# Decode attention with feed-forward: groups of eight heads with two loads for K and V each, and w_gate loaded in three pieces

## The chip, the cores and the metric

The kernel runs on one core of a Trainium2 chip. The metric is device time in microseconds (us) of one execution. Before the change it is 189.06 us (median of four runs, 188.81 to 189.14), so a difference of half a microsecond can be told. Each profile is one execution, whose span is 1.2 to 1.9 us shorter than the time of the same run. On one core a run is marked slow when it is over 1.5% above the fastest run of the same kernel; ratios below use fast runs only.

## The reference, cut to what matters

Two sequences, one new token each. The parts that move bytes are 32 heads of K and V (the last 1,024 positions of each, 192 values per position, bf16) and the weights.

```python
W = min(4096, max(256, Sk // 4))             # 1024
q = (x @ wq).reshape(B, Sq, Hq, Dh)...       # 2 x 32 heads x 192
k = k_cache[:, :, Sk - W:, :]                # v the same
p = softmax(einsum('bhqd,bhkd->bhqk', q, k) * Dh ** -0.5)
o = einsum('bhqk,bhkd->bhqd', p, v) ... @ wo
...                                          # adaLN around both halves
_gelu(x @ w_gate) * (x @ w_up) @ w_down
```

The kernel reads 76.88 MB in all, each byte once. K and V are 50 MB of that (their caches are four times as large; the rest isn't read).

## The kernel before

All large loads are issued by one queue, in one fixed order, into a ring of eight slots and into a region for the other weights. A K or V load brings 128 rows of 12,288 bytes (32 positions of one head), one row to each SBUF partition. The line that says which row goes to which partition:

```python
HQ = 4; PH = P // HQ          # 4 heads in a group, 32 blocks of positions
J = W // PH                   # 32 positions in a block
NQD = H // HQ; NG = B * NQD   # 8 quads, 16 groups
...
quad, b = group(i)
src = A_k_cache if kind == "k" else A_v_cache
return src[b].rearrange("(i u) s d -> u i s d", u=NQD)[quad, :, K0:Sk, :] \
             .rearrange("i (p j) d -> p i (j d)", p=PH), SLOT
```

Read as nested counts, the source is 32 blocks outside, 4 heads inside, 6,144 elements in a row; the destination is 128 partitions. So partition 4p + i gets block p of head i. The head step is 12 MiB, the block step 12,288 bytes.

w_gate is one load of 128 rows:

```python
S.dma("sp", k_dma(wg_v..., B_w_gate.rearrange("(p k) n -> p (k n)", k=KT)), sem_wg, ...)
```

For each group the vector engine multiplies K with q (two multiplies of 128 x 3,072), the matrix engine adds up products, and a chain of small steps makes the softmax.

## Time and profile before

| kernel before | |
|---|---|
| time, median | 189.06 us |
| HBM bytes read | 76.88 MB |
| mean rate over the span | 410 GB/s |
| a 12,288-byte packet on its DMA engine | 464.5 ns |
| vector multiplies | 32 x 1.75 us = 56 us |

From the page of the kernel before: the DMA rows of the 40 slices (busy tenths of the 16 DMA engines, and GB/s), the chain that ended last, the group of the large multiplies (busy us, mean ns, idle us before them and what ended it), and three DMA issues (count, size of one, median us from issue to landing).

```profile
DMA  7999998999999999999999999999999999999991
GB/s 254 402 451 435 430 459 372 422 435 424 430 422 422 427 425 426 427 424 420 419 432 432 422 423 422 421 438 422 424 423 422 419 488 428 416 384 442 398 396 45
...
DMA 71%; DVE 15%; PE 7%; ACT 2%; SPq 2%; issue 1%
...
L490 DVE TENSOR_TENSOR prod<-ring,qbc 128x3072 bf16<-128x3072 bf16 x32 | 55.9, 1751 | 14.3 <-DMA ring<-in_A_k_cache_dram 14.3
...
ring<-in_A_k_cache_dram SPq DMA_DIRECT2D x16, 1536.0 KB, 24.4
ring<-in_A_v_cache_dram SPq DMA_DIRECT2D x16, 1536.0 KB, 24.2
...
r<-in_B_w_gate_dram SPq DMA_DIRECT2D x1, 1920.0 KB, 25.0
```

The DMA engines are busy almost everywhere, at about 425 GB/s. The time from issue to landing is long only because several loads are always queued ahead.

One more reading comes from the trace's records of landings, which the page does not print. A load's 16 parts mark their completion one by one. In the last load of the kernel before, the 16 marks lie between 182.92 and 184.75 us, a spread of 1.83 us. I read each mark as one engine's, since there are 16 of both and the spread comes back in the three loads ahead (1.95, 1.94 and 1.87 us): the engines do not finish together.

### The profile page before, as it was taken

Reading aid. Unit: us, or ns where it says so; the run is one execution under the profiler, and the core shown is the slowest. Engines: PE = TensorE matmul, PEld = TensorE weight load, DVE = VectorE, ACT = ScalarE, POOL = GpSimd, SP = SyncE. Lnnn points to the kernel's source line nnn. Section 1 sums busy time; section 2 is a strip of 40 time slices with the busy share of each in tenths; the row PEclk is TensorE's granted clock in tenths of the full one; section 3 lists DMA queues with packets and bytes.
Section 4 is the critical chain, followed back from the end, with each engine's and each line's share of the span. In section 5 each row is a group of like instructions: output and inputs, shape, how many; then the busy total and the mean of one; then the engine's idle time right before and its main releaser. Section 6 shows DMA issues by size and latency. Waiting matters only on the chain.

```text
span 187.6 us, 2409 instructions
## 1 busy us (share of the span) xinstructions
PE 107.5 (57%) x1039; PEld 51.1 (27%) x1039; DVE 98.2 (52%) x147; ACT 29.9 (16%) x72; POOL 5.1 (3%) x23
## 2 busy tenths in 40 slices
PE   0014730742968887676676655675497395364462
PEld 0011200210323443333423323233253152353121
DVE  6131100019588988886595695775865933003211
ACT  3041100082001221112011110210120103103400
POOL 8200000000000000000000000000000000000000
PEclk9999999997587999999879999999969967569696
DMA  7999998999999999999999999999999999999991
GB/s 254 402 451 435 430 459 372 422 435 424 430 422 422 427 425 426 427 424 420 419 432 432 422 423 422 421 438 422 424 423 422 419 488 428 416 384 442 398 396 45
DMA packets 6518, 77.03 MB, mean 411 GB/s; under 512 B 746, under 2 KB 876, under 8 KB 1516
## 3 DMA queue, kind: packets, MB, share of 16 engines
q1 hardware_dynamic: 6492, 76.88, 97.1%
q8 instruction: 8, 0.13, 0.3%
q10 hardware_dynamic: 16, 0.01, 0.0%
q14 instruction: 2, 0.02, 0.0%
HBM read 76.88 MB, written 0.00 MB: 410 GB/s over the span
## 4 chain that ended last, share of the span: by engine, by line
DMA 71%; DVE 15%; PE 7%; ACT 2%; SPq 2%; issue 1%
DMA ring<-in_A_k_cache_dram 37%; DMA ring<-in_A_wq_dram 17%; DMA r<-in_B_w_down_dram 17%; DVE prod L490 9%; PE ps L502 4%; DVE S_sb L509 4%; PE ps L467 2%; SPq L266 2%; ACT qbc L483 2%; DVE ps L485 1%; DVE M L512 1%; ACT qrow L474 1%; PE ps L526 0%; DVE bcR L519 0%; PE ps L684 0%
## 5 line engine op out<-in xcount | busy, mean ns | idle before, releaser
L490 DVE TENSOR_TENSOR prod<-ring,qbc 128x3072 bf16<-128x3072 bf16 x32 | 55.9, 1751 | 14.3 <-DMA ring<-in_A_k_cache_dram 14.3
L502 PE MATMUL ps<-prod,ident_b 128*128 128x512 bf16 x192 | 52.9, 419 | 14.4 <-DVE prod L490 14.4
L502 PEld LDWEIGHTS ps<-prod,ident_b 128*128 128x128 bf16 x192 | 17.5, 104 | 40.2 <-DVE prod L490 17.5
L509 DVE TENSOR_REDUCE S_sb<-ps 128x32 f32<-128x1024 f32 x16 | 19.3, 1206 | 2.1 <-PE ps L502 2.1
L526 PE MATMUL ps<-bcR,bcL 5*128 5x4 f32 x32 | 6.1, 258 | 21.9 <-DVE bcR L519 21.9
L563 ACT ACTIVATE On<-ps,rden 128x384 bf16<-128x384 f32 x16 | 9.3, 580 | 43.5 <-DVE rden L561 21.1
L551 PE MATMUL ps<-ring,E_sb 128*8 128x384 bf16 x256 | 15.5, 369 | 0.0
L534 ACT ACTIVATE E_sb<-Sb_sb 128x128 bf16<-128x128 f32 x16 | 5.0, 310 | 56.4 <-DVE Sb_sb L531 56.4
L467 PE MATMUL ps<-ring,hT 128*2 128x512 bf16 x60 | 6.7, 626 | 9.8 <-DMA ring<-in_A_wq_dram 8.8
L526 PEld LDWEIGHTS ps<-bcR,bcL 5*128 5x128 f32 x32 | 4.7, 183 | 26.1 <-DVE bcR L519 26.1
L477 DVE CAST qrow<-ps 128x512 bf16<-128x512 f32 x1 | 0.7, 692 | 15.7 <-PE ps L467 15.7
L622 PE MATMUL ps<-ring,oT 128*17 128x160 bf16 x192 | 5.5, 294 | 5.6 <-DMA ring<-in_A_wo_dram 5.6
L531 DVE TENSOR_TENSOR Sb_sb<-S_sb,ps 128x128 f32<-128x128 f32 x16 | 4.6, 287 | 7.6 <-PE ps L526 7.6
L540 PEld LDWEIGHTS ps<-denp,maskc 128*128 128x128 f32 x32 | 7.1, 224 | 3.7 <-ACT E_sb L534 0.9
L641 DVE TENSOR_TENSOR lnt<-ps,modR 128x160 f32<-128x160 f32 x1 | 0.3, 325 | 12.6 <-PE ps L622 12.6
L445 PE MATMUL ps<-r,scT 128*17 128x480 bf16 x40 | 4.3, 597 | 3.9 <-DMA r<-in_w_mod_dram 3.9
L622 PEld LDWEIGHTS ps<-ring,oT 128*17 128x17 bf16 x192 | 4.9, 117 | 6.2 <-DMA ring<-in_A_wo_dram 6.2
L551 PEld LDWEIGHTS ps<-ring,E_sb 128*8 128x8 bf16 x256 | 5.1, 90 | 3.7 <-issue 1.2
L396 PE MATMUL ps<-st,selstat 128*128 128x2 f32 x4 | 0.9, 298 | 8.6 <-ACT sqj L392 8.6
L467 PEld LDWEIGHTS ps<-ring,hT 128*2 128x2 bf16 x60 | 1.7, 114 | 14.7 <-DMA ring<-in_A_wq_dram 9.7
L576 PE MATMUL ps<-On,zsel 128*128 128x96 bf16 x64 | 5.2, 241 | 0.7 <-ACT On L563 0.7
L540 PE MATMUL ps<-denp,maskc 128*128 128x1 f32 x32 | 5.1, 230 | 0.8 <-ACT E_sb L534 0.8
(81 smaller groups left out, 71.2 us busy)
## 6 DMA issues: line engine op xcount, KB each, us to landing
ring<-in_A_k_cache_dram SPq DMA_DIRECT2D x16, 1536.0 KB, 24.4
ring<-in_A_v_cache_dram SPq DMA_DIRECT2D x16, 1536.0 KB, 24.2
r<-in_w_mod_dram SPq DMA_DIRECT2D x1, 4800.0 KB, 14.3
ring<-in_A_wq_dram SPq DMA_DIRECT2D x1, 4608.0 KB, 32.3
ring<-in_A_wo_dram SPq DMA_DIRECT2D x1, 4480.0 KB, 23.4
ring<-in_A_wq_dram SPq DMA_DIRECT2D x1, 3072.0 KB, 21.2
ring<-in_A_wo_dram SPq DMA_DIRECT2D x1, 2720.0 KB, 24.1
r<-in_B_w_gate_dram SPq DMA_DIRECT2D x1, 1920.0 KB, 25.0
```

Of the source, the lines that this page charges most:

```text
L467: last = e.matmul(ps[32 * i:32 * i + B, n, :], lhsT=hT[:, k, :], rhs=wv[:, kk, i, n * QW:(n + 1) * QW], start=(k == 0), stop=(k == KT - 1) ...
L490: S.op("dve", lambda e: e.tensor_tensor(out=prod[:, 2 * (g % 2) + ci, :, :], in0=ring[:, sl, ci * JC * Dh:(ci + 1) * JC * Dh].rearrange("p ...
L502: last = e.matmul(o_ap, lhsT=ident_b[:, :], rhs=prod[:, pz, :, t * GC:(t + 1) * GC], start=(t == 0), stop=(t == NCH - 1))
L509: S.op("dve", lambda e: e.tensor_reduce(out=S_sb[:, z, :], in_=ps[:, 2 * z:2 * z + 2, :].rearrange("p k (j c) -> p (k j) c", c=GC), axis=A ...
L526: S.op("pe", lambda e: e.matmul(ps[:, BK_T, P:P + HQ], lhsT=bcL[:, :], rhs=bcR[:, z, :], start=True, stop=True), reads=[("bcR", z), "bcL"] ...
L531: S.op("dve", lambda e: e.tensor_tensor(out=Sb_sb[:, z, :, :], in0=S_sb[:, z, :].unsqueeze(2).broadcast_to([P, J, HQ]), in1=ps[:, BK_T, P: ...
L534: S.op("act", lambda e: e.activation(out=E_sb[:, z, :, :], in_=Sb_sb[:, z, :, :], func=ACTF.Exp, scale=SCALE, accum_out=denp[:, z:z + 1]), ...
L540: S.op("pe", lambda e: e.matmul(ps[:, BK_T, P + 16:P + 17], lhsT=maskc[:, :], rhs=denp[:, z:z + 1], start=True, stop=True), reads=[("denp" ...
L551: last = e.matmul(ps[32 * i:32 * i + 2 * HQ, BK_O, 0:ON], lhsT=E_sb[:, z, 2 * jp:2 * jp + 2, :].rearrange("p j h -> p (j h)"), rhs=ring[:, ...
L563: S.op("act", lambda e: e.activation(out=On[:, quad % 2, b, :], in_=ps[:, BK_O, 0:ON], func=ACTF.Identity, scale=rden[:, z:z + 1]), reads= ...
L576: last = e.matmul(ps[:, BK_OT, 0:B * NT].rearrange("p (b t) -> p b t", b=B), lhsT=zsel[:, jj, x:x + P], rhs=On[:, quad % 2, :, jj * Dh + d ...
L622: last = e.matmul(ps[32 * i:32 * i + RM, BK_M, 0:DR], lhsT=oT[:, t, :], rhs=wv[:, tl, i, :], start=(t == 0), stop=(t == NT - 1), tile_posi ...
```

## The change

Its intent is twofold. First, eight heads share one pass of small softmax steps, which halves their number. For this a partition holds 64 positions of one of eight heads, and these 64 come in two loads of 32, so that a load keeps its size. Second, w_gate is loaded in two pieces of eight rows and one of 112, meant to give one half of the 16 DMA engines nine of its rows and the other half seven, to even out their finish. (In the trace of the changed kernel each eight-row piece leaves eight landing marks and the 112-row piece 16; which engines these are no record says.)

```diff
-    HQ = 4
+    HQ = 8
     PH = P // HQ
     J = W // PH
+    JS = 32
+    NSUB = J // JS
...
+    WG_SPLIT = [(112, 120), (120, 128), (0, 112)]
...
-        items += [("k", 0)]
-        for g in range(1, NG):
-            items += [("k", g), ("v", g - 1)]
+        items += [("k", sq) for sq in range(NSUB)]
+        for sq in range(NSUB, NG * NSUB):
+            items += [("k", sq), ("v", sq - NSUB)]
...
-            return src[b].rearrange("(i u) s d -> u i s d", u=NQD)[quad, :, K0:Sk, :].rearrange("i (p j) d -> p i (j d)", p=PH), SLOT
+            return src[b].rearrange("(h u) s d -> u h s d", u=NQD)[quad, :, K0:Sk, :].rearrange("h (x s j) d -> s x h (j d)", x=PH, s=NSUB)[sub], SLOT
...
-        S.dma("sp", k_dma(wg_v..., B_w_gate...), sem_wg, writes=["wg"], ...)
+        for ci, (p0, p1) in enumerate(WG_SPLIT):
+            S.dma("sp", k_dma(wg_d[p0:p1, :], wg_s[p0:p1, :]), sem_wg[ci], writes=[("wg", ci)], ...)
```

The source of a K or V load is now 16 blocks outside and 8 heads inside. There are still 128 rows of 12,288 bytes, now with a block step of 24,576 bytes and a head step of 6 MiB. The rest of the diff (cut here) adapts the selection matrices, the order of the loop and the spread of q to eight heads.

More of the change, by code (lines that the diff above doesn't have):

```diff
@@ L149, in bass_adaLN_cond__sliding_block_cached__geglu_ffn__decode_kernel @@
     NG = B * NQD
+    V = HQ // NR
+    JS = 32
+    NSUB = J // JS
     NT = NQ // P
@@ L155, in bass_adaLN_cond__sliding_block_cached__geglu_ffn__decode_kernel @@
     assert DD * NT == Dh and DD * H == P and NR * FR == FC and FC * P == F and DR == KT * 32
-    assert HQ == NR and DD * NQD == 32
+    assert V * NR == HQ and JS * NSUB == J and 2 * HQ <= 32
     SCALE = float(Dh) ** -0.5
@@ L160, in bass_adaLN_cond__sliding_block_cached__geglu_ffn__decode_kernel @@
     JC = 16
-    NCK = J // JC
+    NCK = JS // JC
     GC = 512 // JC
@@ L165, in bass_adaLN_cond__sliding_block_cached__geglu_ffn__decode_kernel @@
     ON = 2 * Dh
-    NPAIR = J // 2
+    NPAIR = JS // 2
     NS = 8
-    SLOT = J * Dh
+    SLOT = JS * Dh
     WQ_SPLIT = [(0, 2), (2, 3)]
@@ L177, in bass_adaLN_cond__sliding_block_cached__geglu_ffn__decode_kernel @@
     HP = P // 2
-    X0 = DD * NQD - 1
+    HS = DD * NQD
+    X0 = HS - 1
     ZW = X0 + P
@@ L182, in bass_adaLN_cond__sliding_block_cached__geglu_ffn__decode_kernel @@
     FT = F // NR
-    assert NQB * QW == NQD * Dh
+    UW = min(2, NQD)
+    QU = UW * Dh
+    NQU = NQD // UW
+    assert NQB * QW == NQ // NR == V * NQD * Dh
     MH = 3 * DR
@@ L211, in bass_adaLN_cond__sliding_block_cached__geglu_ffn__decode_kernel @@
         selrow = sb("selrow", [P, NR, B], BF16)
-        selq = sb("selq", [P, B, P], BF16)
+        selq = sb("selq", [P, B, V, P], BF16)
         ztmp = sb("ztmp", [P, NR, 2, HQ], BF16)
@@ L258, in bass_adaLN_cond__sliding_block_cached__geglu_ffn__decode_kernel @@
         sem_wm = S.sem("d_wm")
-        sem_wg = S.sem("d_wg")
+        sem_wg = [S.sem("d_wg%d" % i) for i in range(len(WG_SPLIT))]
         sem_wu = [S.sem("d_wu%d" % i) for i in range(len(WU_SPLIT))]
@@ L268, in bass_adaLN_cond__sliding_block_cached__geglu_ffn__decode_kernel @@
         items = [("wq", k) for k in range(NWQ)]
-        items += [("k", 0)]
-        for g in range(1, NG):
-            items += [("k", g), ("v", g - 1)]
-        items += [("v", NG - 1)]
+        items += [("k", sq) for sq in range(NSUB)]
+        for sq in range(NSUB, NG * NSUB):
+            items += [("k", sq), ("v", sq - NSUB)]
+        items += [("v", sq) for sq in range((NG - 1) * NSUB, NG * NSUB)]
         items += [("wo", i) for i in range(NWO)]
@@ L302, in ring_src @@
                 return A_wo.rearrange("(p t) n -> p (t n)", t=NT)[:, t0 * D:(t0 + n) * D], n * D
-            quad, b = group(i)
+            g, sub = divmod(i, NSUB)
+            quad, b = group(g)
             src = A_k_cache if kind == "k" else A_v_cache
-            return src[b].rearrange("(i u) s d -> u i s d", u=NQD)[quad, :, K0:Sk, :].rearrange("i (p j) d -> p i (j d)", p=PH), SLOT
+            return src[b].rearrange("(h u) s d -> u h s d", u=NQD)[quad, :, K0:Sk, :].rearrange("h (x s j) d -> s x h (j d)", x=PH, s=NSUB)[sub], SLOT
         def declare_ring(consumed=()):
@@ L341, in bass_adaLN_cond__sliding_block_cached__geglu_ffn__decode_kernel @@
              reads=["ones_b"], writes=["selg"], name="selg")
+        S.op("pool", lambda e: e.memset(selq[:, :, :, :], 0.0), writes=["selq"], name="selq0")
         for b in range(B):
-            S.op("pool", lambda e, b=b: e.affine_select(out=selq[:, b, :].rearrange("p (x h) -> p x h", h=HQ),
-                                                        in_=ones_b[:, 0:1].unsqueeze(2).broadcast_to([P, PH, HQ]),
-                                                        pattern=[[0, PH], [-32, HQ]],
-                                                        compare_op=ALU.is_equal, fill=0.0, base=-b, channel_multiplier=1),
-                 reads=["ones_b"], writes=[("selq", b)], name="selq%d" % b)
+            for v in range(V):
+                S.op("pool", lambda e, b=b, v=v: e.affine_select(out=selq[:, b, v, :].rearrange("p (x i v) -> p x i v", i=NR, v=V)[:, :, :, v],
+                                                                 in_=ones_b[:, 0:1].unsqueeze(2).broadcast_to([P, PH, NR]),
+                                                                 pattern=[[0, PH], [-32, NR]],
+                                                                 compare_op=ALU.is_equal, fill=0.0, base=-b, channel_multiplier=1),
+                     reads=["ones_b"], writes=["selq"], name="selq%d_%d" % (b, v))
         S.op("pool", lambda e: e.affine_select(out=ztmp[:, :, :, :].rearrange("p i q h -> p i (q h)"),
@@ L433, in bass_adaLN_cond__sliding_block_cached__geglu_ffn__decode_kernel @@
              reads=["mask_h"], writes=["maskc"], name="maskc")
-        S.op("dve", lambda e: e.tensor_reduce(out=zsel[:, :, X0:X0 + P].rearrange("p q (h m) -> p q h m", m=32)[:, :, :, 0],
+        S.op("dve", lambda e: e.tensor_reduce(out=zsel[:, :, X0:X0 + P].rearrange("p q (h m) -> p q h m", m=HS)[:, :, :, 0],
                                               in_=ztmp[:, :, :, :].rearrange("p i q h -> p q h i"), axis=AX.X, op=ALU.max),
@@ L478, in bass_adaLN_cond__sliding_block_cached__geglu_ffn__decode_kernel, with f @@
                      reads=[bank(n)], writes=[("qrow", n)], name="q1_evac%d" % n)
-        for u, (n, b) in enumerate((n, b) for n in range(NQB) for b in range(B)):
-            bk = BK_T + u % 4
-            S.op("pe", lambda e, n=n, b=b, bk=bk: e.matmul(ps[:, bk, :], lhsT=selq[:, b, :], rhs=qrow[:, n * QW:(n + 1) * QW], start=True, stop=True),
-                 reads=[("selq", b), ("qrow", n)], writes=[bank(bk)], name="q2_%d_%d" % (n, b))
-            S.op("act", lambda e, n=n, b=b, bk=bk: e.activation(out=qbc[:, b, n * QW:(n + 1) * QW], in_=ps[:, bk, :], func=ACTF.Copy),
+        for z, (n, b) in enumerate((n, b) for n in range(NQU) for b in range(B)):
+            bk = BK_T + z % 4
+            def f(e, n=n, b=b, bk=bk):
+                last = None
+                for v in range(V):
+                    o0 = NQD * Dh * v + n * QU
+                    last = e.matmul(ps[:, bk, 0:QU], lhsT=selq[:, b, v, :], rhs=qrow[:, o0:o0 + QU], start=(v == 0), stop=(v == V - 1))
+                return last
+            S.op("pe", f, reads=["selq"] + [("qrow", m) for m in range(NQB)], writes=[bank(bk)], name="q2_%d_%d" % (n, b))
+            S.op("act", lambda e, n=n, b=b, bk=bk: e.activation(out=qbc[:, b, n * QU:(n + 1) * QU], in_=ps[:, bk, 0:QU], func=ACTF.Copy),
@@ L484, in bass_adaLN_cond__sliding_block_cached__geglu_ffn__decode_kernel, with d_mul @@
                  reads=[bank(bk)], writes=[("qbc", b, n)], name="q2_evac%d_%d" % (n, b))
         S.op("dve", lambda e: e.memset(ps[:, 5:8, :], 0.0), writes=[bank(k) for k in range(5, 8)], name="init_O2")
-        def d_mul(g, ci):
-            quad, b = group(g)
-            sl = slot_of[("k", g)]
-            S.op("dve", lambda e: e.tensor_tensor(out=prod[:, 2 * (g % 2) + ci, :, :],
+        def d_mul(sq, ci):
+            quad, b = group(sq // NSUB)
+            sl = slot_of[("k", sq)]
+            pz = 2 * (sq % 2) + ci
+            S.op("dve", lambda e: e.tensor_tensor(out=prod[:, pz, :, :],
@@ L491, in d_mul @@
                                                   in0=ring[:, sl, ci * JC * Dh:(ci + 1) * JC * Dh].rearrange("p (j d) -> p j d", d=Dh),
                                                   in1=qbc[:, b, quad * Dh:(quad + 1) * Dh].unsqueeze(1).broadcast_to([P, JC, Dh]), op=ALU.mult),
-                 reads=[("ring", sl)] + [("qbc", b, n) for n in range(quad * Dh // QW, ((quad + 1) * Dh - 1) // QW + 1)], writes=[("prod", 2 * (g % 2) + ci)], name="mul%d_%d" % (g, ci))
-        def p_reduce(g, ci):
-            pz = 2 * (g % 2) + ci
+                 reads=[("ring", sl), ("qbc", b, quad // UW)], writes=[("prod", pz)], name="mul%d_%d" % (sq, ci))
@@ L498, in f, with p_reduce @@
+        def p_reduce(sq, ci):
+            pz = 2 * (sq % 2) + ci
             def f(e):
@@ L504, in f, with c_sum, c_max @@
                 return last
-            S.op("pe", f, reads=[("prod", pz), "ident_b"], writes=[bank(pz)], name="red%d_%d" % (g, ci))
-        def c_sum(g):
+            S.op("pe", f, reads=[("prod", pz), "ident_b"], writes=[bank(pz)], name="red%d_%d" % (sq, ci))
+        def c_sum(sq):
+            g, sub = divmod(sq, NSUB)
+            z, w = g % 2, sq % 2
+            S.op("dve", lambda e: e.tensor_reduce(out=S_sb[:, z, sub * JS:(sub + 1) * JS], in_=ps[:, 2 * w:2 * w + 2, :].rearrange("p k (j c) -> p (k j) c", c=GC),
+                                                  axis=AX.X, op=ALU.add),
+                 reads=[bank(2 * w), bank(2 * w + 1)], writes=[("S", z)], name="sum_%d" % sq)
+        def c_max(g):
             z = g % 2
-            S.op("dve", lambda e: e.tensor_reduce(out=S_sb[:, z, :], in_=ps[:, 2 * z:2 * z + 2, :].rearrange("p k (j c) -> p (k j) c", c=GC),
-                                                  axis=AX.X, op=ALU.add),
-                 reads=[bank(2 * z), bank(2 * z + 1)], writes=[("S", z)], name="sum_%d" % g)
             S.op("dve", lambda e: e.tensor_reduce(out=M1[:, z:z + 1], in_=S_sb[:, z, :], axis=AX.X, op=ALU.max),
@@ L541, in p_den, with p_pv @@
                  reads=[("denp", z), "maskc"], writes=[bank(BK_T)], name="den_%d" % g)
-        def p_pv(g):
+        def p_pv(sq):
+            g, sub = divmod(sq, NSUB)
             z = g % 2
-            sl = slot_of[("v", g)]
+            sl = slot_of[("v", sq)]
             def f(e):
@@ L550, in f @@
                     i = jp % NR
+                    j0 = sub * JS + 2 * jp
                     last = e.matmul(ps[32 * i:32 * i + 2 * HQ, BK_O, 0:ON],
-                                    lhsT=E_sb[:, z, 2 * jp:2 * jp + 2, :].rearrange("p j h -> p (j h)"),
+                                    lhsT=E_sb[:, z, j0:j0 + 2, :].rearrange("p j h -> p (j h)"),
                                     rhs=ring[:, sl, 2 * jp * Dh:(2 * jp + 2) * Dh],
-                                    start=(jp < NR), stop=(jp >= NPAIR - NR), tile_position=(0, 32 * i))
+                                    start=(sub == 0 and jp < NR), stop=(sub == NSUB - 1 and jp >= NPAIR - NR), tile_position=(0, 32 * i))
                 return last
-            S.op("pe", f, reads=[("E", z), ("ring", sl)], writes=[bank(BK_O)], name="PV_%d" % g)
+            S.op("pe", f, reads=[("E", z), ("ring", sl)], writes=[bank(BK_O)], name="PV_%d" % sq)
         def c_rec(g):
@@ L581, in p_sel @@
             S.op("pe", f, reads=[("On", quad % 2, bb) for bb in range(B)] + ["zsel"], writes=[bank(BK_OT)], name="sel_%d" % quad)
-        for g in range(NG + 2):
+        for sq in range((NG + 1) * NSUB + 1):
+            g, sub = divmod(sq, NSUB)
             has = g < NG
             prev = 1 <= g <= NG
-            pp = g >= 2
+            head = sub == 0
+            pp = g >= 2 and head
             if has:
-                d_mul(g, 0)
-                p_reduce(g, 0)
+                d_mul(sq, 0)
+                p_reduce(sq, 0)
             if pp:
                 c_rec(g - 2)
-            if prev:
-                c_sum(g - 1)
+            if 1 <= sq <= NG * NSUB:
+                c_sum(sq - 1)
+            if prev and head:
+                c_max(g - 1)
             if has:
-                d_mul(g, 1)
-                declare_ring([("k", g)])
-            if prev:
+                d_mul(sq, 1)
+                declare_ring([("k", sq)])
+            if prev and head:
                 c_max2(g - 1)
@@ L600, in bass_adaLN_cond__sliding_block_cached__geglu_ffn__decode_kernel @@
             if has:
-                p_reduce(g, 1)
-            if prev:
+                p_reduce(sq, 1)
+            if prev and head:
                 c_exp(g - 1)
@@ L607, in bass_adaLN_cond__sliding_block_cached__geglu_ffn__decode_kernel @@
             if prev:
-                p_pv(g - 1)
-                declare_ring([("v", g - 1)])
+                p_pv(sq - NSUB)
+                declare_ring([("v", sq - NSUB)])
         S.op("act", lambda e: e.activation(out=oT[:, :, 0:RM:RB].rearrange("p t b -> p b t"),
@@ L629, in bass_adaLN_cond__sliding_block_cached__geglu_ffn__decode_kernel @@
         r3_dead = [wm_dma] + mod_pe
-        S.dma("sp", k_dma(wg_v.rearrange("p k n -> p (k n)"), B_w_gate.rearrange("(p k) n -> p (k n)", k=KT)), sem_wg,
-              writes=["wg"], deps=r3_dead, name="ld_wg")
+        wg_d, wg_s = wg_v.rearrange("p k n -> p (k n)"), B_w_gate.rearrange("(p k) n -> p (k n)", k=KT)
+        for ci, (p0, p1) in enumerate(WG_SPLIT):
+            S.dma("sp", k_dma(wg_d[p0:p1, :], wg_s[p0:p1, :]), sem_wg[ci], writes=[("wg", ci)], deps=r3_dead, name="ld_wg%d" % ci)
         for ci, (k0, nk) in enumerate(WU_SPLIT):
@@ L657, in f @@
                     return last
-                S.op("pe", f, reads=["ln2_out", key], writes=[bank(bk)], name="ffn_%s%d" % (name, ci))
-        ffn_gu(0, wg_v, "gate", [(0, KT, "wg")])
+                S.op("pe", f, reads=["ln2_out"] + key, writes=[bank(bk)], name="ffn_%s%d" % (name, ci))
+        ffn_gu(0, wg_v, "gate", [(0, KT, [("wg", ci) for ci in range(len(WG_SPLIT))])])
         S.op("act", lambda e: e.activation(out=gl[:, :], in_=ps[:, 0, 0:FT], func=ACTF.Gelu_apprx_tanh),
              reads=[bank(0)], writes=["gl"], name="gelu")
-        ffn_gu(1, wu_v, "up", [(k0, nk, ("wu", ci)) for ci, (k0, nk) in enumerate(WU_SPLIT)])
+        ffn_gu(1, wu_v, "up", [(k0, nk, [("wu", ci)]) for ci, (k0, nk) in enumerate(WU_SPLIT)])
         S.op("dve", lambda e: e.tensor_tensor(out=aR[:, :], in0=ps[:, 1, 0:FT], in1=gl[:, :], op=ALU.mult),
```

## The prediction

> **What bounds the kernel now.** The DMA stream. The page's slices give the 16 engines 9 tenths or more from slice 2 to slice 39, and 410 GB/s over the span (76.88 MB of 187.6 us). The packet records say the same: a 12,288-byte packet takes 464.5 ns (26.5 GB/s on one engine), and all packets' time divided by 16 is about 182 us, from 1.7 us to the last landing at 184.4 us. The chain of waits has 71% DMA and ends with w_down (issued at 152.7, landed at 184.4), then about 3.2 us of last matmuls, two vector operations and the store. Vector work is 98 us, matmuls 107 us. They cost nothing as long as the queue stays fed: K and V are issued some 24 us before they land (table of DMA issues), so several loads are always queued.
>
> **The change, part 1: groups of eight heads.** K and V remain 32 loads of 1,536 KB in 12,288-byte rows, so the stream keeps its bytes and packet sizes. Large multiplies (32 x 1.75 us) and sums (16 x 1.2 us) stay. The small softmax steps run 8 times instead of 16; the subtraction and exp get four times wider each time, so the vector engine saves only a few us. The matrix engine loses some 140 small instructions. All of that is off the critical path: the last up-projection half lands at 180.0, aT is ready at 182.4, the last w_down piece lands only at 184.4. Expected gain: about 0. A side effect: eight 16 KB instruction fetches share the DMA engines and occupy one engine for 1.04 us each. With fewer instructions one may vanish.
>
> **Part 2: w_gate.** In the last load, the 16 engines finish over 1.83 us: six within 0.2 us of the first, seven 1.45 to 1.83 us later, close to what one or two instruction fetches cost. The mean finish is 0.95 us before the last: no balancing can give more. One 15,360-byte row takes 0.58 us. [...]
>
> **The risk.** [...] No record of the kernel before shows such a load. [...] I give this somewhat less than half.
>
> **Time.** 189.0 - 0.6 if balancing works[...]: predicted 188.8 us, 8 in 10 between 187.9 and 190.6. Faster by over 2%: 0.02; within 2%: 0.94; slower: 0.04.
>
> **What would show it.** Right: the stream still full in all slices, K and V landings unchanged, the 16 completion marks of the last w_down load within about 1.3 us instead of 1.83, the chain still ending in w_down. [...] Part 1 neutral: the last V load lands within 0.5 us of its time before.
>
> **What would make it wrong.** A row order in HBM that slows packets (mean above 470 ns); the queue running dry early, because V is now issued one group later; or compute becoming the last wait at the end.

Terms are cut from this where no trace or run shows them: which engines take which rows of w_gate, and what would slow eight rows to neighbouring partitions (112 to 119, and 120 to 127), the load that "The risk" means. The full sum came to this. If the split relieves the late engines of one 15,360-byte row (0.58 us in the trace), the end comes 0.5 to 0.6 us earlier, 189.0 - 0.6 = 188.4 us; if not, 0.3 to 0.6 us later. If the eight-row loads are slow, it comes 1 to 2 us later, up to 191 us; that was my guess, with no measurement behind it. The 188.8 us weigh these cases.

## More of the kernel before

The windows view, for 60 to 140 us, deep inside the K and V stretch, ends with granted clock, DMA share and GB/s:

```profile
60.00:140.00 80.00, 54.89 (x440) 27.29 (x439) 61.19 (x83) 11.42 (x36) 0.00 (x0) 0.96 1.01 426
```

So the DMA stream bounds the kernel: 426 GB/s, with the vector engine busy 61 of 80 us.

## The result, and the profile after

The changed kernel takes 307.74 us (median of four, 304.6 to 310.11) against 189.06. The ratio is 1.6225 (95% interval 1.6105 to 1.6346). A ratio here is the mean time of one kernel's fast runs over that of the other's of the same rounds, so it is not quite the ratio of the medians quoted. The profiled run, 310.11 us, is marked slow, being 1.8% above the fastest; the three fast runs are 304.6 to 307.8, so the packet figures below, which come from the slow one, can be off by about a per cent, and nothing rests on that. The output passed the comparison.

The same lines of the page of the changed kernel:

```profile
DMA  8999999999999999999999999999999999999993
GB/s 319 418 458 442 207 215 218 218 220 223 210 222 212 222 216 222 220 217 222 214 220 218 223 220 215 222 214 223 222 215 223 215 222 242 339 430 288 221 349 153
...
DMA 41%; another core or an unknown queue 32%; DVE 20%; PE 4%; SPq 2%; issue 1%
...
L508 DVE TENSOR_TENSOR prod<-ring,qbc 128x3072 bf16<-128x3072 bf16 x32 | 56.0, 1752 | 117.4 <-DMA ring<-in_A_k_cache_dram 117.4
...
ring<-in_A_k_cache_dram SPq DMA_DIRECT2D x16, 1536.0 KB, 52.6
ring<-in_A_v_cache_dram SPq DMA_DIRECT2D x16, 1536.0 KB, 55.3
...
r<-in_B_w_gate_dram SPq DMA_DIRECT2D x1, 1680.0 KB, 40.7
```

And its window of 60 to 140 us:

```profile
60.00:140.00 80.00, 36.39 (x191) 12.90 (x191) 30.26 (x29) 3.33 (x8) 0.00 (x0) 0.70 1.01 218
```

The DMA engines are as busy as before, but they move 218 GB/s instead of 426. The low rate begins and ends with the K and V loads (slice 5 to slice 34), rises during wo (339, 430), and drops again with w_gate (288, 221). The multiplies themselves are unchanged, 1,752 ns each; they wait 117.4 us for K instead of 14.3. (The w_gate line is the largest of its three loads now, 112 rows.) This also explains the entry "another core or an unknown queue": only one core runs, and in the timeline these pieces stand just ahead of multiplies that the group above shows waiting for K. The chain view could not name the load.

A busy DMA row is thus no sign of a good rate. What tells it is the duration of packets of one size, from the trace's packet records:

| packet (bytes) | used by | count | before, mean ns | after, mean ns |
|---|---|---|---|---|
| 12,288 | K, V | 4,096 | 464.5 | 904.4 |
| 15,360 | w_gate | 128 | 578.5 | 1,180.8 |
| 9,216 | first part of w_up | 128 | 354.0 | 494.7 |
| 24,576 | first part of wq | 128 | 912.0 | 912.0 |

The K and V packets alone account for (904.4 - 464.5) ns x 4,096 / 16 engines = 112.6 us of the 118.7 us. The wq packets, which come before K, are untouched.

### The profile page after: what moved, and what is told of

Read it like the earlier page. It is cut to its first block, busy times and chain, and to the rows that moved or that the text cites. A ratio compares the mean times of both kernels' runs of the same rounds, so it can differ in the third digit from the quotient of the medians.

```text
span 308.3 us, 2212 instructions
## 1 busy us (share of the span) xinstructions
PE 129.3 (42%) x969; PEld 51.1 (17%) x969; DVE 96.3 (31%) x115; ACT 23.5 (8%) x46; POOL 5.9 (2%) x26
## 4 chain that ended last, share of the span: by engine, by line
DMA 41%; another core or an unknown queue 32%; DVE 20%; PE 4%; SPq 2%; issue 1%
DMA r<-in_B_w_down_dram 15%; DMA ring<-in_A_k_cache_dram 15%; DVE prod L508 13%; DMA ring<-in_A_wq_dram 12%; DVE S_sb L528 4%; SPq L274 2%; DVE Sb_sb L553 1%; PE ps L478 1%; PE ps L548 1%; PE ps L520 1%; DVE bcR L541 0%; DVE M L534 0%; PE ps L575 0%; PE ps L713 0%
## 5 line engine op out<-in xcount | busy, mean ns | idle before, releaser
L520 PE MATMUL ps<-prod,ident_b 128*128 128x512 bf16 x192 | 74.6, 552 | 105.1 <-DVE prod L508 104.7
L508 DVE TENSOR_TENSOR prod<-ring,qbc 128x3072 bf16<-128x3072 bf16 x32 | 56.0, 1752 | 117.4 <-DMA ring<-in_A_k_cache_dram 117.4
L520 PEld LDWEIGHTS ps<-prod,ident_b 128*128 128x128 bf16 x192 | 21.6, 126 | 149.6 <-DVE prod L508 119.1
L575 PE MATMUL ps<-ring,E_sb 128*16 128x384 bf16 x256 | 16.3, 385 | 11.6 <-DMA ring<-in_A_v_cache_dram 11.6
L587 ACT ACTIVATE On<-ps,rden 128x384 bf16<-128x384 f32 x8 | 4.6, 581 | 168.0 <-DVE rden L585 141.1
L575 PEld LDWEIGHTS ps<-ring,E_sb 128*16 128x16 bf16 x256 | 5.4, 95 | 20.0 <-DMA ring<-in_A_v_cache_dram 16.5
L556 ACT ACTIVATE E_sb<-Sb_sb 128x512 bf16<-128x512 f32 x8 | 5.0, 630 | 42.5 <-DVE Sb_sb L553 42.5
L553 DVE TENSOR_TENSOR Sb_sb<-S_sb,ps 128x512 f32<-128x512 f32 x8 | 5.5, 687 | 4.7 <-PE ps L548 4.7
L548 PE MATMUL ps<-bcR,bcL 9*128 9x8 f32 x16 | 3.9, 317 | 4.2 <-DVE bcR L541 4.2
L684 PE MATMUL ps<-r,h2T 128*2 128x384 bf16 x40 | 4.0, 488 | 3.5 <-DMA r<-in_B_w_gate_dram 2.3
L548 PEld LDWEIGHTS ps<-bcR,bcL 9*128 9x128 f32 x16 | 3.2, 247 | 8.9 <-DVE bcR L541 8.9
```

The costliest lines, as they stand in the source:

```text
L508: S.op("dve", lambda e: e.tensor_tensor(out=prod[:, pz, :, :], in0=ring[:, sl, ci * JC * Dh:(ci + 1) * JC * Dh].rearrange("p (j d) -> p j ...
L520: last = e.matmul(o_ap, lhsT=ident_b[:, :], rhs=prod[:, pz, :, t * GC:(t + 1) * GC], start=(t == 0), stop=(t == NCH - 1))
L548: S.op("pe", lambda e: e.matmul(ps[:, BK_T, P:P + HQ], lhsT=bcL[:, :], rhs=bcR[:, z, :], start=True, stop=True), reads=[("bcR", z), "bcL"] ...
L553: S.op("dve", lambda e: e.tensor_tensor(out=Sb_sb[:, z, :, :], in0=S_sb[:, z, :].unsqueeze(2).broadcast_to([P, J, HQ]), in1=ps[:, BK_T, P: ...
L556: S.op("act", lambda e: e.activation(out=E_sb[:, z, :, :], in_=Sb_sb[:, z, :, :], func=ACTF.Exp, scale=SCALE, accum_out=denp[:, z:z + 1]), ...
L575: last = e.matmul(ps[32 * i:32 * i + 2 * HQ, BK_O, 0:ON], lhsT=E_sb[:, z, j0:j0 + 2, :].rearrange("p j h -> p (j h)"), rhs=ring[:, sl, 2 * ...
```

## The experiments

**Theories.** One theory, P, and four rivals:

- *Theory P (partitions).* The order of a load's rows decides which partitions the engines write at the same moment, and in some orders these writes hold each other up. Then 16 blocks outside and 8 heads inside would be such an order, and so would eight rows to neighbouring partitions. When the expectations were written this was a guess: no record names the engine or the partition of a packet.
- *Rival H (HBM).* The new steps of 24,576 bytes and 6 MiB are slow to read.
- *Rival C.* The grouped computation holds up the loads.
- *Rival L.* For w_gate, three loads cost more than one. *Rival K:* a load on only eight engines (eight landing marks instead of 16) is slow as such.

Ten kernels ran. Where a result is wrong (other rows of K and V, or in another order), the comparison still passed: it cannot tell which K and V rows were used. That does not matter for their times.

### 1. The new HBM steps in the old order (e1_hbm_steps)

```diff
-return src[b].rearrange("(i u) s d -> u i s d", u=NQD)[quad, :, K0:Sk, :].rearrange("i (p j) d -> p i (j d)", p=PH), SLOT
+return src[b].rearrange("(a i u) s d -> a u i s d", i=HQ, u=HQ)[quad // HQ, quad % HQ, :, Sk - 2 * W:Sk, :].rearrange("i (p s j) d -> s p i (j d)", p=PH, s=2)[b], SLOT
```

> The kernel before, with the HBM addresses of its K and V loads changed to the steps of the changed kernel (24,576 bytes from one row to the next, 6 MiB from head to head) but still 32 rows outside and 4 heads inside. Its result is wrong on purpose. Theory P[...]: 189 us, 12,288-byte packets at about 464 ns. Rival H (the HBM row steps are slow): about 300 us, packets at about 900 ns. Rival C (the grouping of the computation holds the loads up): 189 us.

Measured: 188.98 us, ratio 1.0002 (0.9989 to 1.0016). Its window of 60 to 140 us:

```profile
60.00:140.00 80.00, 55.27 (x440) 27.27 (x441) 60.59 (x81) 11.78 (x36) 0.00 (x0) 0.96 1.01 425
```

The packets took 464.3 ns. The new steps in HBM cost nothing. H falls.

### 2. The new order with the old HBM steps (e2_order16x8)

```diff
-return src[b].rearrange("(i u) s d -> u i s d", u=NQD)[quad, :, K0:Sk, :].rearrange("i (p j) d -> p i (j d)", p=PH), SLOT
+return src.rearrange("b (i u) s d -> u (b i) s d", u=NQD)[quad, :, K0:Sk, :].rearrange("h (s x j) d -> s x h (j d)", s=2, j=J)[b], SLOT
```

> The kernel before, with its old HBM steps (12,288 bytes from row to row, 12 MiB from head to head) but 16 rows outside and 8 heads inside in each K and V load, eight heads being four of each batch. Same bytes, each row read once, wrong result on purpose; the computation is the old one. Theory P[...]: about 300 us, packets at about 900 ns. Rival H (HBM steps): 189 us, 464 ns. Rival C (grouping): 189 us.

Measured: 298.06 us (292.44 to 302.35), ratio 1.5589 (1.5487 to 1.5691). Two of the four runs, the profiled one among them, are marked slow; the ratio is that of the two fast ones. Its window:

```profile
60.00:140.00 80.00, 37.65 (x186) 15.81 (x187) 30.43 (x40) 5.49 (x16) 0.00 (x0) 0.65 1.01 219
```

The packets took 894.1 ns. The old kernel, with its old computation, the same rows read once each and the same steps, falls to half the rate by the order 16 by 8 alone.

### 3. The grouped computation with the old loads (e3_eight_old_loads)

```diff
-g, sub = divmod(i, NSUB)
-quad, b = group(g)
+quad, b = divmod(i, B)
 ...
-return src[b].rearrange("(h u) s d -> u h s d", u=NQD)[quad, ...].rearrange("h (x s j) d -> s x h (j d)", x=PH, s=NSUB)[sub], SLOT
+return src[b].rearrange("(i u) s d -> u i s d", u=8)[quad, :, K0:Sk, :].rearrange("i (p j) d -> p i (j d)", p=32), SLOT
```

> The changed kernel with only the source of its K and V loads set back to that of before (32 rows outside, 4 heads inside, old HBM steps); computation in groups of eight and the split w_gate load stay; wrong result on purpose. Theories P and H: 188 to 192 us, packets at 464 ns, what is over 189 being the w_gate split. Rival C: stays near 300 us.

Measured: 197.16 us, ratio 1.0418 (1.0384 to 1.0451). K and V packets were back at 464.4 ns. C falls. The 8 us that remain were more than the expected 3, and belong to w_gate: its packets took 1,161.5 ns here.

### 4. The split of w_gate alone (e4_gate_split)

The kernel before with `WG_SPLIT` of the change and nothing else (same diff lines as above).

> The kernel before with nothing but the split w_gate load. If balancing the engines works: 188.4 to 188.6 us and last marks within 1.3 us. Theory P[...]: 190 to 192 us, the packets of the eight-row loads over 1 us each instead of 0.58 us.

Measured: 196.18 us, ratio 1.0378 (1.0357 to 1.0399): 7.3 us lost, well over what I expected under P. First the window that holds w_gate in the kernel before, then in this one:

```profile
168.00:175.00 7.00, 2.06 (x94) 1.76 (x98) 2.33 (x9) 2.98 (x5) 0.00 (x0) 0.96 1.00 417
```

```profile
168.00:182.00 14.00, 3.96 (x102) 3.15 (x102) 2.50 (x10) 3.20 (x5) 0.00 (x0) 0.59 1.01 220
```

417 GB/s became 220, for twice as long. Not only the 16 packets of the two eight-row loads were slow: all 128 packets of w_gate took 1,162 ns in the mean, against 578.5 before. The load of 112 rows is slow by itself: the landing marks put the end of both eight-row loads at 175.79 us, and the 42 packets of w_gate that started later took 971 to 1,148 ns, 1,060 in the mean. Out of w_gate comes (1,162 - 578.5) ns x 128 / 16 = 4.7 us. The first part of w_up, behind it, adds (517 - 354) x 128 / 16 = 1.3 us. Some 1.3 us of the 7.3 stay unexplained.

Theory P, as I applied it, does not account for the 112 rows. I looked for a collision in the eight-row loads alone and expected about 578 ns for these; after 175.79 us no packet took less than 971. Whether their partitions are the cause too, or something else, is open.

### 5. The change without the split (f1_eight_plain_gate)

```diff
-    WG_SPLIT = [(112, 120), (120, 128), (0, 112)]
+    WG_SPLIT = [(0, 128)]
```

> The changed kernel with w_gate loaded whole again (one load of 128 rows); everything else of the change stays. Theory P[...]: the split cost 7.3 us in the kernel before, so about 300 us here, against 307.7 with it; the K and V packets stay near 900 ns, the 15,360-byte packets return to about 580 ns. If the two parts were not independent (the split mattering more behind slow K and V loads), the difference would be far from 7 us.

Measured: 298.59 us (295.66 to 299.61), ratio 1.577 (1.5691 to 1.5849). The w_gate packets took 579.6 ns, K and V 890 ns. The order of K and V costs 298.59 - 188.89 = 109.7 us, and the split 307.74 - 298.59 = 9.2 us behind it, against 7.3 alone. The two separate costs, 109.7 + 7.3, make 117.0 of the 118.7 us.

### 6. The same loads behind three small ones (f2_skew)

If P is right, engines collide because of what they write at the same time, and then it should help to run them out of step, with nothing changed in the K and V loads. Three small loads of unused data ahead of K are meant to do that. They have 12, 8 and 4 as their outer count and four rows of 12,288 bytes inside. I assumed that each gives packets to some engines only, as the eight-row loads with their eight landing marks do, so that the engines start K some packets apart; which engines they load is not shown. (The first multiply also waits for them.)

```diff
 # on top of f1_eight_plain_gate, in the loop that issues the ring's loads:
+if it == ("k", 0):
+    for z, (n, p0) in enumerate([(12, 32), (8, 80), (4, 112)]):
+        far = A_v_cache[0, 0:n, 0:8 * JS, :].rearrange("h (c t j) d -> t h c (j d)", c=4, t=2)[0]
+        S.dma("sp", k_dma(prod[p0:p0 + 4 * n, 0:2, :, :]..., far), sem_skew[z], writes=[("skew", z)], ...)
```

> The same as f1_eight_plain_gate, plus three small loads just ahead of the first K load, whose data nobody uses[...]. [...] K and V loads keep their addresses, their order and their 16 by 8 shape; 1.2 MB more is moved[...]. Theory P[...]:[...] packets fall to about 464 to 600 ns and the time to 195 to 230 us. Theory H or any other that blames addresses, row order in HBM or the cost of descriptors: no better than f1, about 300 to 306 us.

Measured: 243.8 us (median of four, 233.51 to 251.7). Three of the four runs are marked slow, the profiled one among them, so no ratio was computed. The one fast run, 233.51 us, is 65 us below f1's median of 298.59, and even the slowest, 251.7, is 44 us below f1's fastest, 295.66, although 1.2 MB more is moved. From its page the GB/s of the slices, and then the window of 60 to 140 us, first of f1, then of this run:

```profile
GB/s 295 424 437 416 462 208 198 283 308 295 310 304 320 315 285 304 327 302 338 330 317 316 312 340 320 336 321 295 304 304 310 303 233 284 408 408 418 387 102 14
```

```profile
60.00:140.00 80.00, 35.01 (x191) 12.63 (x189) 28.79 (x28) 3.33 (x8) 0.00 (x0) 0.72 1.01 222
```

```profile
60.00:140.00 80.00, 45.90 (x235) 17.51 (x233) 40.48 (x39) 4.63 (x11) 0.00 (x0) 0.71 1.01 314
```

The rate is some 310 GB/s during K and V, where f1 had 222 and the changed kernel 218. The packets took 653 ns in the mean. They spread widely, from 460 ns, the full speed of the kernel before, up to over 900. So the same K and V loads run much faster behind three small loads that are meant to shift the engines against each other. A theory that charges each address, row or descriptor by itself does not explain that. One rival is left by this run: the shift also changes which rows are read from HBM at the same moment, so reads that collide in HBM would be relieved too. No run here varies the partitions of the K and V loads alone; run 10 does it for a small load. My number was too good: I expected at most 230 us, and only part of the loss came back. Why is open: the records name neither an engine nor a partition, so I can't say how the small loads shifted the engines, or which still met.

### 7. The grouping alone (f3_eight_only)

e3 with the whole w_gate load (`WG_SPLIT = [(0, 128)]`).

> Grouping alone: the changed kernel's computation in groups of eight, with the old source of the K and V loads (wrong result on purpose) and the whole w_gate load. Theory P: the DMA stream is that of before, so 188.6 to 189.3 us; seven 16 KB instruction fetches or fewer instead of eight may give up to 0.4 us. If the grouped computation had a cost of its own: over 190 us.

Measured: 189.1 us, ratio 1.0007 (0.9994 to 1.0019). In the window of 60 to 140 us:

```profile
60.00:140.00 80.00, 52.28 (x374) 21.09 (x363) 59.72 (x60) 7.09 (x16) 0.00 (x0) 0.94 1.01 425
```

The grouping costs nothing and brings nothing. It saves 1.5 us of vector work in these 80 us, beside a full DMA stream. One of the eight instruction fetches of 16 KB that share the DMA engines is gone (seven packets in the page's instruction queue), also without a visible gain. So there is no better kernel to be had by repairing the order of loads under the groups of eight.

### 8. Another order that keeps the rate (f4_order64x2)

```diff
-return src[b].rearrange("(i u) s d -> u i s d", u=NQD)[quad, :, K0:Sk, :].rearrange("i (p j) d -> p i (j d)", p=PH), SLOT
+return src[b].rearrange("(a i u) s d -> a u i s d", i=2, u=NQD)[0, quad, :, Sk - 2 * W:Sk, :].rearrange("i (p j) d -> p i (j d)", p=2 * PH), SLOT
```

> The kernel before with 64 rows outside and 2 heads inside in each K and V load (old steps of 12,288 bytes and 12 MiB; wrong result on purpose). Theory P does not fix the outcome[...]. A theory that blames heads inside a row block (eight far addresses per outer row) expects 189 us.

Measured: 189.0 us, ratio 1.0004 (0.999 to 1.0017), packets at 464.4 ns. So a 12,288-byte packet takes 464.4 ns with an outer count of 64 and 464.5 with 32, but 904.4 with 16. A packet of w_gate (15,360 bytes) takes 578.5 ns with 128 outside, which is the same full rate (26.6 bytes per ns against 26.5), but 1,162 when it is cut to 112 rows and two times 8. P did not say on which side 64 would fall (I put 189 us if it behaves as 32, about 298 if as 16), so this run does not test it. It also shows that an inner count of 2 is as harmless as 4. Eight heads inside never ran without 16 blocks outside; but f2 leaves the eight heads in place and gets faster, so they can't be the whole cause.

### 9. w_gate in three loads by columns (g1_gate_by_columns)

```diff
-    WG_SPLIT = [(112, 120), (120, 128), (0, 112)]
+    WG_SPLIT = [(0, 480), (480, 960), (960, 7680)]
...
-            S.dma("sp", k_dma(wg_d[p0:p1, :], wg_s[p0:p1, :]), ...
+            S.dma("sp", k_dma(wg_d[:, p0:p1], wg_s[:, p0:p1]), ...
```

(on top of e4_gate_split)

> The kernel before with w_gate in three loads of the same sizes as in the change (1/16, 1/16 and 14/16 of it) but cut by columns, 128 rows each. Theory P (which partitions an engine's rows go to): 188.7 to 189.3 us. Rival L (more and smaller loads, or three semaphores, cost the time): 192 to 196 us, as the cut by rows did.

Measured: 189.1 us, ratio 1.0001 (0.9977 to 1.0025). Three loads of the same sizes, cut so that each has all 128 rows, are free. L falls.

### 10. Two probes of the same eight rows (g2_two_probes)

```diff
+far = B_w_gate.rearrange("(p k) n -> p (k n)", k=KT)[0:8, :]
+S.dma("sp", k_dma(probe[0:32:4, 0:7040], far[:, 0:7040]), sem_probe[0], ...)     # ahead of w_gate
 S.dma("sp", ... w_gate, one load of 128 rows ...)
+S.dma("sp", k_dma(probe[112:120, 0:7168], far[:, 0:7168]), sem_probe[1], ...)    # behind it
```

(`probe` is scratch; the rows differ in length so that the trace can tell them apart.)

> The kernel before with two eight-row loads of unused data added, from the same eight rows of HBM: one of 14,080-byte rows to partitions 0, 4, 8 ... 28 just ahead of w_gate, one of 14,336-byte rows to partitions 112 to 119 just behind it. [...] Theory P: the first one's packets take about 530 ns like any other[...], the second one's over 1,000 ns[...]. Rival K (a load on eight engines is slow as such): both slow. [...] Time: 189.5 to 193 us.

(If the premise of the split holds, I expected the first probe's eight landing marks within 0.3 us of the earliest marks of the load ahead plus one packet.)

Measured: 191.54 us, ratio 1.0123 (1.0092 to 1.0155). The packet records give, in ns in order of start:

```
to partitions 0, 4, ... 28 (14,080 bytes):   532 528 526 529 533 538 539 536
to partitions 112 to 119  (14,336 bytes):    566 656 720 1046 874 892 742 878
```

The same eight rows of HBM, eight packets each: full speed to spread partitions, 533 ns in the mean, and 797 ns to neighbouring ones. K falls, and for this load the cause is the partitions written, not what is read from HBM. The second row was milder than the 1,000 ns and more that I expected, perhaps because the eight packets did not start together: four between 173.4 and 173.7 us, four between 175.1 and 176.9.

The second probe's packets were not the only slow ones. At 174.5 us all 16 packets in flight were slow: one of the probe (1,046 ns), eight of w_gate (1,274 to 1,676, where 578 is usual) and seven of w_up (941 to 1,102, where 354 is). From 174 to 176 us the rate was 179 GB/s, against 396 in the kernel before. So packets of the other loads were slow beside those of the eight neighbouring rows; how one load could hold up all the others is not shown.

The landing marks of the first probe also test the premise of the split. The split can help only if the engines that take an eight-row load are early ones. The probe is such a load; that the two of the split go to the same eight engines is assumed. Less one packet of 0.53 us, its marks stand at:

```
first probe's eight, marks less 0.53:    168.81 168.86 168.93 169.04   169.67 169.76   170.28 170.90
all 16, in the load ahead (wo):          seven at 168.80-169.05, three at 169.65-169.74, six at 170.28-171.28
```

Four of the probe's eight are early, two in the middle, two late. By subtraction the other eight have three early, one in the middle and four late. The late engines are not just those that the probe leaves out, in this execution at least, which up to the first probe is the kernel before. The split had little to even out, even where it costs nothing.

## Why the prediction was wrong

- **"The DMA stream bounds the kernel": right**, and the reason why the loss went fully into the time. 112.6 us more of packet time for each engine became 118.7 us more in all, together with w_gate.
- **"K and V remain 32 loads of 1,536 KB in 12,288-byte rows, so the stream keeps its bytes and packet sizes ... Expected gain: about 0": this step failed.** The premise is true: the count of 12,288-byte packets is 4,096 in both traces. The conclusion is not: the same packets went from 464.5 to 904.4 ns. I took a packet's time as a function of its size. The runs show that it also depends on the order of a load's rows: the order alone, in the old kernel, made 298.06 us (e2), and the same loads behind the three small ones came to 243.8 (f2). That the order acts through the partitions that the engines write at the same moment is theory P: that the partitions count is shown for an eight-row load (g2), and for K and V it is inferred.
- **The risk in the partitions was seen, but looked for only in the two small loads.** I asked it of the eight-row loads of w_gate and not of the largest loads of the diff, whose source had changed its outer count in plain view. The check that the runs suggest is to write down, for each changed load, the outer and inner counts and the partitions of its rows, and to time alone those that are new.
- **w_gate: the risk was rightly seen, its reach was not.** I counted a slowdown in the two small loads only, 1 to 2 us in all (the guess named beside the prediction); alone the split cost 7.3 us (e4). The missing term is the third load: 112 rows, which I counted at full speed. All 128 packets slowed, from 578.5 to 1,162 ns, and w_up behind them from 354 to 517 ns. What explains that is open.
- **The premise of the split, that one half of the engines is late: not so** for the halves that the first probe shows (g2: four early and two late in one, three and four in the other).
- **Grouping off the critical path: right.** f3 gives 189.1 us against 188.89.
- **One instruction fetch fewer: right** (seven instead of eight), worth nothing that can be measured.
- **"A row order in HBM that slows packets (mean above 470 ns)"** stood in the list of what could make the prediction wrong. The sign was right, but the steps in HBM were not the cause: the new ones in the old order gave 464.3 ns and 188.98 us (e1).

What is shown: the loss is in the order of rows within loads, not in addresses, loads' sizes or count, or computation; for an eight-row load it depends on the partitions written (g2), and for K and V small loads ahead, meant to shift the engines, relieve it in part (f2). What is inferred: that the partitions written together are the cause for K and V; no record names an engine's partitions. What stays unexplained: the 112-row load (e4) and the reach of the second probe (g2).

## What to carry to other kernels

When a load's access pattern changes, compare not only bytes and row length but also the outer count of the source. In this kernel 32, 64 and 128 outside, over 128 partitions, ran at about 425 GB/s; 16 outside, or a cut to 112 rows, ran at about 220. A DMA row that reads 9 tenths in both cases, at 218 as at 426 GB/s, can't show the loss; GB/s in a window and the duration of packets of one size do. Before shifting rows between DMA engines to even out their finish, measure with a small marked load whether the engines that take it are early, and cut by columns rather than by rows (189.1 us against 196.18 for w_gate here).
